# Reordered closing work in a cached attention decode step: maxima, last weights and the last half of V

## Chip, cores, metric

One core of a Trainium2 chip. The profile's span, from first to last instruction, is about 1.9 us shorter than that time.

## The reference

```python
# A_x (1,1,448); A_k_cache, A_v_cache (1,16,65536,256); all bf16
x  = A_x
xn = _layernorm(x)
q  = (xn @ wq) split into 16 heads of 256
p  = softmax(q . k_cache * 256**-0.5)          # over 65536 keys, per head
s  = (p . v_cache, heads side by side) @ wo    # 4096 x 448
g  = silu(silu(xn @ w1) @ w2)                  # the gate
return x + s * g
```

One query against 16 heads of 65536 keys: 1.07 GB of keys and values are read once, with hardly any reuse.

## The kernel before

K and V stream through three large buffers in blocks of 16384 keys of one head (64 blocks of 8 MB each for K and for V). VectorE and ScalarE form the scores, ScalarE the exponentials, and TensorE multiplies them with V. The rows of each block are joined at the end through their maxima and sums. The change concerns only what follows the loops: the last blocks, whose V comes in pieces, and the output projection, whose weights `wo` come in pieces too.

```python
vn = cuts(0, 32, 64, 96, 128)                 # V of the last block but one, in pieces (keys per partition)
vz = cuts(0, 32, 64, 96, 112, 120, 128)       # V of the last block
pieces = cuts(0, 5, 10, 14, 16)               # wo, by heads
# order of the transfers (SP, one queue):
#   K last (2 halves), vn 0..3, vz 0..1, wo 0, wo 1, vz 2.., wo 2, wo 3
...
def pe_rows():    # maxima of the partitions put into one row (L330 before)
def pe_bcast():   # the maximum sent to all partitions (L336)
def pe_turn():    # the O row, copied out of PSUM by act_out, turned into columns (L346)
def pe_keys():    # V matmuls, 128 x 2 x 512 (L318)
def project():    # 1 x 448 projections with wo, two for a head (L681)
...
pe_block(NBLK - 3, 0)
pe_turn()
pe_v(1)                                  # V of the block before, all 128 keys
pe_max(NBLK - 2)                         # pe_rows, query, pe_bcast
...
keys(psO, 2, 2, vn, nl, 0, 3, True)      # keys() waits for each piece, then multiplies it
pe_rows()
keys(psO, 2, 2, vn, nl, 3, 4, False, od)
pe_bcast()
... # ScalarE: softmax of the first half of the last block, sums of the second
keys(psO2, 0, 1, vz, zl, 0, 2, True, od)
pe_turn()
pe.wait_ge(wl[0], 16); project(*pieces[0])
pe_rows()
pe.wait_ge(wl[1], 16); project(h0, h0 + 3)
pe_bcast()
project(h0 + 3, h1)
... # softmax of the last half; sums; weights of the last head
keys(psO, 0, 1, vz, zl, 2, 3, True)      # the last half of V: first piece,
pe_turn()                                # a turn between,
keys(psO, 0, 1, vz, zl, 3, len(vz), False, od)
act_out()
pe.wait_ge(wl[2], 16); project(*pieces[2])
pe_turn(tok=True)
... # VectorE: last head's output (L750)
pe.wait_ge(wl[3], 16); project(pieces[3][0], H1)
project(H1, H)                           # then VectorE: * gate, + x; store
```

## Time and profile before

| | before |
|---|---|
| time, three executions | 2524.33 us median (2523.97 to 2526.91) |
| span of the profiled execution | 2520.7 us |
| read from HBM | 1084 MB, 430 GB/s over the span |
| last V piece of 2 MB (keys 64 to 96) lands | 2504.90 us |
| TensorE without idle time | 2504.95 to 2516.63 us |

VectorE is busy 89% of the span, but, as the prediction reads from the page, it is the transfers that set the pace (416 to 436 GB/s in each of the first 39 slices).

### The profile page before, as it was taken

The numbers are of one execution on the slowest core, as the hardware profiler recorded it, in microseconds if no ns is written. First come the engines' busy times: TensorE is split into PE (matmuls) and PEld (weight loads), VectorE is DVE, ScalarE is ACT, GpSimd is POOL, SyncE is SP. The second block draws the span as 40 slices with busy tenths as digits, with TensorE's granted clock in tenths as the row PEclk, the third lists the DMA queues.
The fourth block names the chain that finished last, engine by engine and source line by source line (L and its number), as shares of the span: only waits on it lengthen the run. The fifth ranks groups of instructions, "written<-read, shape, count | busy, mean of one in ns | idle before, by whom it ended". The sixth has DMA issues, their size and how long they took to land. (4 is left out here: it accounts for less than half of the span.)

```text
span 2520.7 us, 29977 instructions
## 1 busy us (share of the span) xinstructions
PE 1198.9 (48%) x5125; PEld 500.4 (20%) x5125; DVE 2233.5 (89%) x10281; ACT 1443.8 (57%) x6992; POOL 2.5 (0%) x13
## 2 busy tenths in 40 slices
PE   3353544545535445445354354453553544535557
PEld 2121211212212112112121121121221211212123
DVE  6989889889898898898898988988989889889897
ACT  4656556556565565565555655655656556556564
POOL 0000000000000000000000000000000000000000
PEclk7676767767767667677676676776767767767779
DMA  9999999999999999999999999999999999999998
GB/s 423 416 433 432 434 436 433 434 433 433 433 433 433 433 434 432 433 434 434 435 436 434 435 436 435 433 433 434 433 433 433 433 433 433 433 433 434 433 432 342
DMA packets 22728, 1084.52 MB, mean 430 GB/s; under 512 B 2354, under 2 KB 4532, under 8 KB 4916
## 3 DMA queue, kind: packets, MB, share of 16 engines
q1 hardware_dynamic: 22706, 1084.30, 99.6%
q8 instruction: 6, 0.10, 0.0%
q14 instruction: 14, 0.11, 0.0%
q10 hardware_dynamic: 2, 0.00, 0.0%
HBM read 1084.29 MB, written 0.00 MB: 430 GB/s over the span
## 5 line engine op out<-in xcount | busy, mean ns | idle before, releaser
L271 ACT ACTIVATE R<-R 128x256 bf16<-128x256 bf16 x3328 | 1330.7, 401 | 698.5 <-ACTq L154 698.5
L249 DVE CUSTOM_DVE_ANT_0 R<-R,qcur 128x256 bf16<-128x256 bf16 x4864 | 1699.8, 416 | 0.0
L318 PE MATMUL bank<-R,PV 128*2 128x512 bf16 x4096 | 1025.5, 417 | 25.3 <-DMA R<-in_A_v_cache_dram 11.5
L238 DVE TENSOR_TENSOR R<-R,qcur 128x3328 bf16<-128x3328 bf16 x256 | 482.6, 1885 | 197.2 <-DVEq L154 197.1
L271 ACT ACTIVATION_READ_ACCUMULATOR R<-R 128x1 f32 x3328 | 620.1, 186 | 0.0
L330 PE MATMUL bank<-ident,rmax 128*1 128x128 bf16 x65 | 17.1, 263 | 1022.4 <-PEq L154 1022.4
L318 PEld LDWEIGHTS bank<-R,PV 128*2 128x2 bf16 x4096 | 365.7, 90 | 657.2 <-issue 207.1
L249 DVE DVE_READ_ACCUMULATOR2_ANT S<- 128x1 f32 x4864 | 379.4, 78 | 0.0
L346 PE MATMUL bank<-eye,O 2*128 2x1 f32 x536 | 97.2, 298 | 239.8 <-PEq L154 239.8
L330 PEld LDWEIGHTS bank<-ident,rmax 128*1 128x1 bf16 x65 | 5.2, 79 | 1026.6 <-issue 1026.2
L346 PEld LDWEIGHTS bank<-eye,O 2*128 2x128 f32 x536 | 93.3, 255 | 257.8 <-issue 257.8
L284 ACT ACTIVATE hist<-bank 128x1 f32 (+1 forms) x65 | 11.1, 171 | 206.3 <-ACTq L154 206.3
L305 ACT COPY hist<-bank 128x2 f32 (+1 forms) x66 | 10.6, 160 | 119.2 <-ACTq L154 119.2
L214 DVE TENSOR_REDUCE gmax<-bank 1x1 bf16<-1x128 f32 x65 | 18.3, 281 | 38.6 <-DVEq L154 38.6
L231 DVE CAST qcur<-bank 128x256 bf16<-128x256 f32 x64 | 27.2, 425 | 16.0 <-DVEq L154 14.3
L297 ACT COPY O<-bank 2x512 f32<-2x512 f32 x67 | 37.4, 559 | 5.7 <-ACTq L154 5.7
L286 ACT ACTIVATE PV<-S,hist 128x128 bf16<-128x128 f32 (+1 forms) x65 | 26.0, 400 | 13.4 <-ACTq L154 13.1
L358 PE MATMUL bank<-q,ident 16*128 16x256 bf16 x63 | 24.4, 387 | 0.0
L224 DVE COPY S<-S 128x128 f32<-128x128 f32 (+1 forms) x65 | 14.7, 226 | 9.5
L225 DVE TENSOR_REDUCE rmax<-S 128x1 bf16<-128x128 f32 (+1 forms) x65 | 18.2, 280 | 0.0
L336 PE MATMUL bank<-gmax,ones_row 1*128 1x1 bf16 x65 | 10.3, 159 | 16.0 <-PEq L154 16.0
L336 PEld LDWEIGHTS bank<-gmax,ones_row 1*128 1x128 bf16 x65 | 6.5, 100 | 33.4 <-issue 33.4
(65 smaller groups left out, 101.8 us busy)
## 6 DMA issues: line engine op xcount, KB each, us to landing
R<-in_A_k_cache_dram SPq DMA_DIRECT2D x4, 4096.0 KB, 24.7
R<-in_A_v_cache_dram SPq DMA_DIRECT2D x7, 2048.0 KB, 24.1
R<-in_A_wq_dram SPq DMA_DIRECT2D x1, 3072.0 KB, 12.9
R<-in_A_wo_dram SPq DMA_DIRECT2D x2, 1120.0 KB, 19.3
R<-in_B_w_dram SPq DMA_DIRECT2D x1, 1568.0 KB, 27.1
R<-in_B_w_dram SPq DMA_DIRECT2D x1, 1344.0 KB, 5.8
R<-in_A_v_cache_dram SPq DMA_DIRECT2D x1, 1024.0 KB, 15.7
R<-in_A_v_cache_dram SPq DMA_DIRECT2D x2, 512.0 KB, 16.9
```

What stands on the lines that cost most here:

```text
L214: dve.reduce_max(out=gmax[0:1, :], in_=ps_m[0:1, :], axis=AX.X).then_inc(gm, 1)
L225: dve.reduce_max(out=rmax[:, :], in_=S[:, c0:c1], axis=AX.X).then_inc(rm, 1)
L231: dve.tensor_copy(out=qcur[:, :], in_=ps_q).then_inc(sd, 1)
L238: m = dve.tensor_tensor(out=pair, in0=pair, in1=qcur[:, None, :].to_broadcast([P, NA, Dh]), op=ALU.mult,)
L249: ins = dve.tensor_tensor_reduce(out=Kv[:, c, :], in0=Kv[:, c, :], in1=qcur[:, :], scale=1.0, scalar=0.0, op0=ALU.mult, op1=ALU.add, accum ...
L271: ins = act.activation(out=prod, in_=prod, func=ACT.Identity, accum_out=S[:, c : c + 1],)
L286: act.activation(out=PV[s][:, c0:c1], in_=S2[:, c0:c1], func=ACT.Exp, bias=col(0, 1), scale=scale, accum_out=col(1, 2),).then_inc(pv, 1)
L297: act.copy(out=O[:, :], in_=po).then_inc(oc, 1)
L318: ins = pe.matmul(po, lhsT=PV[t][:, c : c + 2], rhs=R[s][:, c * Dh : (c + 2) * Dh], start=(start and c == k0), stop=(stop and c == k1 - 2),)
L330: pe.matmul(ps_m[0:1, :], lhsT=rmax[:, 0:1], rhs=ident[:, :], start=True, stop=True).then_inc(tm, 1)
L346: ins = pe.matmul(ps_t[:, a : a + 1], lhsT=Ov[:, j, a, :], rhs=eye2[:, j : j + 1], start=(j == 0), stop=(j == 1),)
L358: pe.matmul(ps_q, lhsT=ident[0:H, at(h)].to_broadcast([H, P]), rhs=q16[:, :], start=True, stop=True,).then_inc(qr, 1)
```

## The change

Its intent is to take work off TensorE's path behind the last large V piece. (1) The row of maxima of the last block's first half is made behind two pieces of V, not three, and its broadcast ahead of the fourth. (2) A turn moves into a wait, and only four projections stand ahead of the row of maxima of the second half, so that the last softmax and the last head's weights are ready sooner, ahead of the gate. (3) The last half of V, cut finer, is multiplied in one go in the order in which it lands, with no turn between; the other turn goes between the projections.

```diff
--- before.py
+++ after.py
@@ -170,7 +170,7 @@
         return tuple(zip(c[:-1], c[1:]))
 
     vn = cuts(0, 32, 64, 96, 128)
-    vz = cuts(0, 32, 64, 96, 112, 120, 128)
+    vz = cuts(0, 32, 64, 80, 96, 112, 120, 128)
     nl = [sem(f"nl{t}") for t in range(len(vn))]
     zl = [sem(f"zl{t}") for t in range(len(vz))]
     pieces = cuts(0, 5, 10, 14, 16)
@@ -706,10 +706,11 @@
                 pe_keys(po, t, s, k0, k1, start and n == a, last and done is not None,
                         done if last else None)
 
-        keys(psO, 2, 2, vn, nl, 0, 3, True)
+        keys(psO, 2, 2, vn, nl, 0, 2, True)
         pe_rows()
+        keys(psO, 2, 2, vn, nl, 2, 3, False)
+        pe_bcast()
         keys(psO, 2, 2, vn, nl, 3, 4, False, od)
-        pe_bcast()
         act_softmax(LAST, 0, 0, HK)
         act_sums(0, 2)
         act_out()
@@ -718,33 +719,33 @@
 
 
         take(pe, pv)
-        keys(psO2, 0, 1, vz, zl, 0, 2, True, od)
+        keys(psO2, 0, 1, vz, zl, 0, 1, True)
         pe_turn()
+        keys(psO2, 0, 1, vz, zl, 1, 2, False, od)
+        act_out(psO2)
         need("pe", t_o)
         pe.wait_ge(wl[0], 16)
-        project(*pieces[0])
+        (h0, h1) = pieces[0]
+        project(h0, h0 + 2)
         pe_rows()
-        pe.wait_ge(wl[1], 16)
-        (h0, h1) = pieces[1]
-        project(h0, h0 + 3)
+        project(h0 + 2, h1)
         pe_bcast()
-        project(h0 + 3, h1)
         act_softmax(LAST + 1, 0, HK, KB)
-
+        pe_turn()
         take(pe, pv)
         t15 = pe_sums(ps_m[:, 0:NL], N1, NENT)
         weights(N1, NENT, H1, H, (ps_m[:, 0:NL], t15))
-        act_out(psO2)
-        keys(psO, 0, 1, vz, zl, 2, 3, True)
-        pe_turn()
+        t_r = mark("act", act_row(LAST))
         t_g = silu(g_t, ps_y, g_e, t_y)
-        t = mark("act", act_row(LAST))
-        need("dve", t)
+        need("dve", t_r)
         outputs(N1, NENT - 1, H1, H, NL - 1)
-        keys(psO, 0, 1, vz, zl, 3, len(vz), False, od)
+        pe.wait_ge(wl[1], 16)
+        project(*pieces[1])
+        keys(psO, 0, 1, vz, zl, 2, len(vz), True, od)
         act_out()
         pe.wait_ge(wl[2], 16)
-        project(*pieces[2])
+        (h0, h1) = pieces[2]
+        project(h0, h0 + 2)
         t = pe_turn(tok=True)
         need("dve", t)
         t_l = mark("dve", dve.scalar_tensor_tensor(
@@ -755,6 +756,7 @@
             op0=ALU.mult,
             op1=ALU.add,
         ))
+        project(h0 + 2, h1)
         pe.wait_ge(wl[3], 16)
         project(pieces[3][0], H1)
         need("pe", t_l)
```

## The prediction

> **What bounds the kernel now.** I read the page first, then the chain that ended last, then TensorE's timeline of the last 30 us, then the issues and landings of the last transfers.
>
> The page, part 2 (40 slices of 63 us each):
>
> ```profile
> DMA  9999999999999999999999999999999999999998
> GB/s 423 416 433 432 434 436 433 434 433 433 433 433 433 433 434 432 433 434 434 435 436 434 435 436 435 433 433 434 433 433 433 433 433 433 433 433 434 433 432 342
> ```
>
> All 39 first slices move 416 to 436 GB/s with the DMA engines 90% busy or more. 1084 MB must be read (keys and values), and the change moves no byte of it. So about 2504 of 2520.7 us of the span stand, whatever the engines do; only the tail behind the last transfers can shrink. The chain that ended last shows the tail:
>
> ```profile
> 2479.93 24.97 DMA R<-in_A_v_cache_dram
> 2504.91 0.04 issue
> 2504.95 3.61 PE bank L318 x16
> 2508.57 1.03 PE bank L346 x8
> 2509.59 3.54 PE bank L318 x16
> 2513.14 1.51 PE bank L681 x8
> 2514.65 1.03 PE bank L346 x8
> 2515.68 0.95 PE bank L681 x4
> 2516.63 0.02 issue
> 2516.66 0.62 DVE R L763
> 2517.28 0.02 issue
> 2517.30 0.61 DVE x_f L765
> ```
>
> The third piece of the last V block (keys 64 to 96, 2 MB) lands at 2504.90. From there TensorE is never idle until 2516.6: 16 V matmuls, a "turn" (the O row turned into columns, L346), 16 more V matmuls, 8 projections (L681), a second turn, 4 projections. Then two VectorE steps and the store, 4.0 us to the end. TensorE, not DMA, sets these 11.7 us. TensorE's timeline just before it:
>
> ```profile
> 2494.02 3.61 PE L318 MATMUL bank<-R,PV 128*2 128x512 bf16 x16 [2.34 <-DMA R<-in_A_v_cache_dram]
> 2497.56 1.10 PE L346 MATMUL bank<-eye,O 2*128 2x1 f32 x8
> 2498.59 2.05 PE L681 MATMUL bank<-R,OT 128*1 128x448 bf16 x10
> 2500.48 0.22 PE L330 MATMUL bank<-ident,rmax 128*1 128x128 bf16 x1
> 2500.54 1.30 PE L681 MATMUL bank<-R,OT 128*1 128x448 bf16 x6
> 2501.77 0.17 PE L336 MATMUL bank<-gmax,ones_row 1*128 1x1 bf16 x1
> ```
>
> The row of maxima (L330) runs at 2500.48, though VectorE's timeline has its input (L225) finished at 2499.60: it stood behind a turn and ten projections. The broadcast (L336) stood behind six more, although the maximum was ready at 2501.13.
>
> The last transfers: the two V pieces' halves of 512 KB land 16.5 and 17.2 us after their issues (about 2492.2 and 2492.7), so at 2508.7 and 2509.9; the 1 MB piece before them (issued 2491.65, 15.7 us) at 2507.35. The output weights `wl[2]`, issued at 2493.20:
>
> ```profile
> DMA to landing us min/median/max: 18.9/18.9/18.9
> ```
>
> land at 2512.1, and `wl[3]` (issued 2494.3) at 2513.2. In the kernel before nobody waits for them: TensorE reaches them at 2513.14. The stretches show why they are so late:
>
> ```profile
> 2510.50:2511.00 0.50, 0.50 (x4) 0.17 (x2) 0.00 (x0) 0.00 (x0) 0.00 (x0) 1.00 0.18 68
> 2511.00:2512.20 1.20, 1.20 (x7) 0.50 (x6) 0.00 (x0) 0.00 (x0) 0.00 (x0) 1.00 0.07 25
> ```
>
> The DMA share is 0.07, about one engine of 16[...].
>
> [...] the trace has 2507.35 - 2504.90 = 2.45 us, and I use that. [...] The trace's 3.54 us for 16 is 221 ns at clock 1.00[...]. [...]
>
> **The change part by part.** Work is nearly constant: 32 V matmuls, 20 projections, all turns remain; no turn is added or removed, but one leaves the tail.
>
> Step 1, maxima of the last block's first half. They go behind two pieces of V instead of three: L330 at about 2479.1 (its input ends 2478.98) instead of 2481.73. VectorE waited 0.40 us at L214 for it; it now starts the second half 0.40 us earlier, so the second half's maxima end near 2499.2. The broadcast goes ahead of the fourth piece, so ScalarE's softmax starts near 2483 instead of 2487.0; it removes ScalarE as a limit (it ends its sums about 1 us sooner), but VectorE's 0.40 is all that reaches TensorE. Estimates.
>
> Step 2, the last weights. The psO turn goes into the wait before 2494.02 (idle there is 2.34 us, it needs 1.03): free. Only 4 projections remain ahead of L330 (2497.6 to 2498.4), so L330 is bound by its input: 2499.25, gain 1.2 us. Then 6 projections to about 2500.6 and the broadcast at 2500.65 instead of 2501.77. ScalarE's softmax then ends near 2501.7; the turn of psO2 fits beside it (2500.8 to 2501.8). The sums matmul L668 follows at 2501.85 (2502.94 before) and ends about 2502.2. The ten projections of `pieces[1]`, now behind it: 10 x 0.19 = 1.9 us, to 2504.1.
>
> Step 3, the V half in landing order. The split pieces land at 2504.90 - 2.45 = 2502.45 and at 2504.90. TensorE starts 32 matmuls at 2504.1 with no turn among them: 32 x 0.221 = 7.1 us, to 2511.2. Each piece is there when needed: the second at 2505.9 (lands 2504.9), the third at 2507.6 (2507.35, tight), the last two at 2509.4 and 2510.3 (2508.7, 2509.9). Before, this ended at 2513.14: gain 1.9 us, of which 1.03 is the turn and 0.85 the earlier start.
>
> Step 4, the new wait. At 2511.2 TensorE meets `wl[2]`, which lands at 2512.1: 0.9 us idle, so half of step 3 is given back. The copy of O (L297, 0.57 us) hides in it. Then 4 projections 0.75, turn 1.03, 4 projections 0.75 (VectorE's L751, 0.23 us, hides behind them), 2 with `wl[3]` 0.38, the last 2 0.38: 3.3 us, with 0.05 for waits to 2515.5. Before: 2516.63. **Sum: 1.1 us earlier**, and the 4.0 us behind it stand. VectorE's silu, 2.94 us of it the reciprocal, ends about 2508 and is not in the way.
>
> 2524.33 - 1.1 = 2523.2 us, 0.04%.
>
> **The rivals.**
> (a) No DMA wait takes the place: if TensorE alone set the tail, it would end at 2511.2 + 3.3 = 2514.5, gain 2.1 us, 2522.2. Against it: the landing at 2512.1, which the order of transfers doesn't change.
> (b) [...] The waits before V pieces end at 2478.28, 2483.17, 2488.07, 4.9 us apart, but the next at 2494.02, 5.95[...]. One such loss more or one at another place, or the cost of one more transfer, moves `wl[2]`'s landing by about as much: gain 0 to 0.1, 2524.2; one less, gain near 2, 2522.3.
> (c) The earlier weights don't come: if VectorE, or L330's new place behind fewer projections, leaves L668 at 2502.94, the ten projections end at 2505.2, V at 2512.3, after `wl[2]`; the tail ends at 2515.6. Then still 1.0 us. This makes the estimate robust: steps 1 and 2 are nearly hidden by step 4.
> (d) Softer effects: TensorE's clock falls in the added idle time before L330. It is 1.00 from 2480 on, with idle times over 2 us, so I give this little weight.
>
> **Range and chances.** The effect lies between 0 and 2 us. The three runs before spread from 2523.97 to 2526.91, and the profiled one took 2522.64: run to run noise is larger than the effect. So 2523.2, with 2521.5 to 2525.3 for 8 in 10. Faster or slower by 2% means 50 us, which no part of a 40 us closing can give unless the stream of transfers itself is disturbed, and it is untouched: faster 0.003, same 0.992, slower 0.005.
>
> **What would show it right or wrong.** Page part 2 unchanged in its first 39 slices. L330 near 2479.1 and 2499.3, L668 near 2501.9, the V matmuls of the last half in one stretch of about 7.1 us without a turn, from about 2504.1; then an idle time of TensorE near 0.9 us ahead of L681 put down to `in_A_wo_dram`; a chain that ended last which now begins with that transfer instead of V's; last L681 ending near 2515.5. If the wait is not there, (a); if it is longer than 1.5 us and the span is not shorter, (b); if L668 is late, (c). A change above 5 us either way, or slices of lower GB/s, would mean that the closing disturbs the transfers in a way I have not seen.

The sum is 1.1 us, worked with 2.45 us between two landings of the trace (of the 2 MB piece at 2504.90 and of the 1 MB piece at 2507.35) and with 221 ns for a V matmul.

## More of the kernel before

The metric is the device time of one execution in microseconds.

The page's first part (busy time of each engine) and the TensorE clock in the 40 slices of its second part:

```profile
PE 1198.9 (48%) x5125; PEld 500.4 (20%) x5125; DVE 2233.5 (89%) x10281; ACT 1443.8 (57%) x6992; POOL 2.5 (0%) x13
PEclk7676767767767667677676676776767767767779
```

The clock row is in tenths of full speed: TensorE runs at 0.711 in the mean of the span, and is busy for 48% of it.

## The result and the profile after

2523.26 us median of four (2521.99 to 2526.62), before 2524.15 (2523.65 to 2526.91). The ratio is 0.9996, with a 95% interval from 0.9979 to 1.0014: the same, as forecast. The 0.9 us between the medians is about the size forecast (1.1), but smaller than the spread of either kernel. The traces had to show whether it came in the way foretold.

The chain that ended last, in the first profile of the changed kernel (in order of time: start us, us, what; the two steps of VectorE at its end are left out):

```profile
2495.02 17.86 DMA R<-in_A_wo_dram
2512.87 0.04 issue
2512.92 0.92 PE bank L681 x4
2513.84 1.03 PE bank L346 x8
2514.86 2.67 PE bank L681 x8
2517.53 0.02 issue
```

TensorE's timeline before it:

```profile
2494.68 3.61 PE L318 MATMUL bank<-R,PV 128*2 128x512 bf16 x16 [0.27 <-DMA R<-in_A_v_cache_dram]
2499.05 0.22 PE L330 MATMUL bank<-ident,rmax 128*1 128x128 bf16 x1
...
2501.50 0.36 PE L668 MATMUL bank<-hist,ones_sq 128*128 128x5 f32 x2
...
2503.68 3.87 PE L318 MATMUL bank<-R,PV 128*2 128x512 bf16 x16
2508.18 3.61 PE L318 MATMUL bank<-R,PV 128*2 128x512 bf16 x16 [0.64 <-DMA R<-in_A_v_cache_dram]
2512.92 0.92 PE L681 MATMUL bank<-R,OT 128*1 128x448 bf16 x4 [1.12 <-DMA R<-in_A_wo_dram]
```

The order came as meant. The row of maxima is at 2499.05 (2500.48 before), the sums at 2501.50 (2502.94), and the last half of V begins at 2503.68 (2504.95), has no turn in it, and is done about 2511.8 (2513.1). The chain now begins with the output weights, for which TensorE waits 1.12 us. But the last projections end at 2517.53, and before at 2516.63. Part of that is a later arrival of everything: the piece with keys 32 to 64, the same transfer in both kernels, was there at 2494.68 and at 2494.02. To compare profiles I therefore measure the **stretch**: from the start of the V matmuls on keys 32 to 64, which every kernel here but one (told below) begins when they land, to the end of the last projection. Before it is 2516.63 - 2494.02 = 22.61 us, in this profile 22.85: nothing gained. The last eight projections take 2.67 us, where 1.51 had been forecast, and the profile by stretches says why (busy time of the engines, then TensorE's clock in the third column from the right):

```profile
2514.00:2515.00 1.00, 1.00 (x10) 0.88 (x10) 0.01 (x1) 0.00 (x0) 0.00 (x0) 1.00 0.00 0
2515.00:2516.00 1.00, 1.00 (x5) 0.41 (x4) 0.21 (x1) 0.00 (x0) 0.00 (x0) 0.63 0.00 0
2516.00:2517.50 1.50, 1.50 (x5) 0.26 (x2) 0.00 (x0) 0.00 (x0) 0.00 (x0) 0.50 0.00 0
```

The granted clock falls to half at about 2515.3, 2.3 us behind the end of the new wait. Before, it stayed at 1.00 until TensorE was done. The traces of these two kernels show two values of the clock, 1.00 and 0.50, and in each of them all 128 spans from one change to the next are whole multiples of 3.41 us. What TensorE did in such stretches is read from the traces below. This gave a theory and its rivals, at this point my guesses.

**Theory A**: the wait of 1.1 us that the change makes lowers the clock, and the fall costs 1.2 us, all the gain. **Rival B**: it was a chance of that one profile, of where these stretches of 3.41 us fell in the work. **Rival C**: turns and one-row projections lower it, not the wait. Beside these there was the question which of the three parts helps at all, and why single executions are slow.

### The profile page after: what moved, and what is told of

Read it like the earlier page. It is cut to its first block, busy times and chain, and to the rows that moved or that the text cites. A ratio compares the mean times of both kernels' runs of the same rounds, so it can differ in the third digit from the quotient of the medians.

```text
span 2521.6 us, 29978 instructions
## 1 busy us (share of the span) xinstructions
PE 1203.5 (48%) x5125; PEld 501.3 (20%) x5125; DVE 2233.6 (89%) x10281; ACT 1443.9 (57%) x6992; POOL 2.5 (0%) x13
## 5 line engine op out<-in xcount | busy, mean ns | idle before, releaser
L330 PE MATMUL bank<-ident,rmax 128*1 128x128 bf16 x65 | 17.1, 263 | 1022.1 <-PEq L154 1022.0
L249 DVE DVE_READ_ACCUMULATOR2_ANT S<- 128x1 f32 x4864 | 385.8, 79 | 0.0
L330 PEld LDWEIGHTS bank<-ident,rmax 128*1 128x1 bf16 x65 | 5.2, 79 | 1027.0 <-issue 1026.9
```

The costliest lines, as they stand in the source:

```text
L249: ins = dve.tensor_tensor_reduce(out=Kv[:, c, :], in0=Kv[:, c, :], in1=qcur[:, :], scale=1.0, scalar=0.0, op0=ALU.mult, op1=ALU.add, accum ...
L330: pe.matmul(ps_m[0:1, :], lhsT=rmax[:, 0:1], rhs=ident[:, :], start=True, stop=True).then_inc(tm, 1)
```

## The experiments

| kernel | executions, us | median | before, median of the same call | stretch in the profile, us |
|---|---|---|---|---|
| before | (4 in the first call, 9 in each other) | | | 22.61 |
| changed, first profile | 4 | 2523.26 | 2524.15 | 22.85 (clock fell) |
| changed, again | 5 | 2522.13 | 2523.39 | 21.77 |
| wait filled | 5 | 2522.50 | 2523.39 | 21.84 |
| weights split | 5 | 2521.31 | 2523.39 | 20.75 |
| weights split, again | 5 | 2521.49 | 2523.16 | 20.60 |
| split, idle times filled | 5 | 2521.33 | 2523.16 | 21.28 |
| split, earlier maxima | 5 | 2521.30 | 2523.22 | 20.70 |
| long wait | 1 | 2525.70 | 2523.16 | 24.96 (clock fell) |
| long wait filled | 1 | 2524.51 | 2523.16 | 23.58 |
| third part alone | 1 | 2522.60 | 2523.39 | 22.19 (clock fell earlier) |
| third part alone, again | 1 | 2522.67 | 2523.22 | 21.94 |
| first two parts alone | 1 | 2524.24 | 2523.22 | 22.64 |

All gave correct results. Kernels are compared only within the same rounds. Every timed comparison has an interval that contains 1, as single slow executions of 2 to 4 us spread both sides. The profiles are few: the kernel before has one, and the two of the split kernel, which is the same twice, differ by 0.15 us.

**The changed kernel again.** No edit.

> The changed kernel unaltered, to see whether its profile repeats. Theory A (the wait for the output weights of the third piece lowers the granted TensorE clock to half, and the last eight projections take 2.7 instead of 1.5 us): again an idle time near 1.1 us ahead of the projections and the clock at 0.5 in their last microsecond; from the start of the V matmuls of keys 32 to 64 to the end of the last projection 22.8 us, as in the first profile of the changed kernel (22.85; 22.61 before). Rival B[...]: the clock stays at 1.00 and the same stretch takes 21.6 us. Time 2523 +- 1 us, 0 to 1 us under the kernel before.

The end of its chain:

```profile
2512.54 0.92 PE bank L681 x4
2513.46 1.03 PE bank L346 x8
2514.49 1.62 PE bank L681 x8
```

The same wait (1.15 us), and the clock stayed at 1.00: the last eight projections took 1.62 us, the stretch 21.77. So the wait doesn't lower the clock each time: Theory A's numbers missed, Rival B's held (21.6). What was left of A: that the wait makes the fall possible. This is what the change is worth when the clock stays at 1.00: 22.61 - 21.77 = 0.84 us.

**The wait filled.** Five matmuls whose result nobody reads, into a bank that is free by then:

```diff
+for _ in range(5):
+    pe.matmul(bank[7][0:2, :], lhsT=PV[0][:, 0:2], rhs=R[1][:, 0 : 2 * Dh], start=True, stop=True)
 pe.wait_ge(wl[2], 16)
```

> Five V matmuls with no use are written to a free bank ahead of the wait for the third piece of output weights, 5 x 0.221 = 1.1 us, in the idle time. Theory A: the clock stays at 1.00 to the end, the last eight projections take 1.5 us, and the stretch from the V matmuls of keys 32 to 64 to the last projection takes 21.6 to 21.8 us, 1.1 us less than in the changed kernel; time about 2522. If the clock falls because of the turns and the one-row projections and not because of the wait (rival C), it falls here too and the stretch stays at 22.8.

Clock 1.00 to the end, stretch 21.84, eight projections in 1.62 us. That agrees with Theory A, but as the unfilled kernel had just shown the same, it tells nothing apart. A larger dose was needed.

**A longer wait, unfilled and filled.** TensorE waits for the fourth piece of `wo` ahead of the projections of the third; in the second kernel ten unread matmuls stand ahead of it.

```diff
+# second kernel only: 10 matmuls as above
 pe.wait_ge(wl[2], 16)
+pe.wait_ge(wl[3], 16)
```

> The changed kernel with the wait made longer: TensorE waits for the fourth piece of output weights too, before the projections of the third, so it is idle 2.2 to 2.3 us instead of 1.1. Theory A: the clock falls to 0.5[...], and the 3.3 us of work behind the wait take 4.3 us or more. If the throttle doesn't answer to the wait, they take 3.3 us at clock 1.00 and the stretch from the V matmuls of keys 32 to 64 is 22.8 us.

> The same long wait, filled with ten V matmuls of no use (2.2 us). Theory A: the clock stays at 1.00, the 3.3 us of work take 3.3 us and the stretch is 22.8 us. Rival C (turns and one-row projections lower the clock): the same as with the unfilled wait.

TensorE's timeline behind the wait, unfilled:

```profile
2514.01 0.92 PE L681 MATMUL bank<-R,OT 128*1 128x448 bf16 x4 [2.33 <-DMA R<-in_A_wo_dram]
2514.86 1.70 PE L346 MATMUL bank<-eye,O 2*128 2x1 f32 x8
2516.49 3.15 PE L681 MATMUL bank<-R,OT 128*1 128x448 bf16 x8
```

and filled:

```profile
2514.92 0.92 PE L681 MATMUL bank<-R,OT 128*1 128x448 bf16 x4
2515.77 1.10 PE L346 MATMUL bank<-eye,O 2*128 2x1 f32 x8
2516.80 1.68 PE L681 MATMUL bank<-R,OT 128*1 128x448 bf16 x8
```

The same twelve projections and turn took 5.64 us behind 2.33 us of idle time, with the clock at 0.5 from 2515.1 on, and 3.57 us behind busy matmuls, at 1.00. The turns and one-row projections are the same, so they alone don't lower it. (The filled kernel's stretch, 23.58, missed its 22.8: in that execution the last V matmuls began late for a reason told below, and the unread ones ran to 2515.09, while the DMA share was 0.00 from 2514.0 on.) The pair isn't clean, as in the filled kernel that late start had also taken away the 0.61 us of idle time between the V matmuls.

The traces tell more. As the clock changes only at multiples of 3.41 us, each trace can be cut into windows of that length, counted back from its last change. V matmuls of 512 columns start 216 ns apart at clock 1.00, 0.42 ns a column; with that, a streaming time can be added up from the packed traces for each window: columns times 0.42 ns (twice that at clock 0.50). In the traces of the kernel before and of the changed kernel's first profile, 603 windows are at full clock. All 130 with 1.232 us of streaming or less were followed by half clock, and all 473 with 1.247 us or more by full clock. That is a count of these two traces, not a limit tested by a run. The windows at the wait, of the changed kernel's first profile (two lines; the second up to the last projection) and of its second profile (two lines):

```profile
2511.85:2515.26 3.41, 2.34 (x15) 1.51 (x16) 0.23 (x1) 0.57 (x1) 0.00 (x0) 1.00 0.03 13
2515.26:2517.53 2.27, 2.26 (x7) 0.51 (x4) 0.00 (x0) 0.00 (x0) 0.00 (x0) 0.50 0.00 0
2508.81:2512.22 3.41, 2.58 (x12) 0.78 (x10) 0.00 (x0) 0.57 (x1) 0.00 (x0) 1.00 0.51 189
2512.22:2515.63 3.41, 3.09 (x19) 1.85 (x20) 0.23 (x1) 0.00 (x0) 0.00 (x0) 1.00 0.02 7
```

In the first profile 1.07 us of the wait and the whole turn (1.03 us, matmuls of one column, which add next to nothing to the count) lie in one window, and 1.22 us of streaming are left. In the second a window ends inside the wait, and its two windows hold 2.41 and 1.97 us. So by this count, at a wait of 1.1 us it is neither the wait (Theory A) nor the turn (Rival C) alone, but both in one window, and where the windows lie decides that (Rival B). In the unfilled long wait, whose clock fell at 2515.1, 2.32 us of idle time lie in one window with 0.75 us of streaming, so there, by the count, the wait is enough. No run here sets the windows' place. By the same count (an estimate from its trace) the kernel before can lose the clock too: a window that ended between 2504.61 and 2506.18 would have put its last V matmuls at half.

**The output weights split.** If the wait is the bound, its landing should be moved, not filled.

```diff
-pieces = cuts(0, 5, 10, 14, 16)
+pieces = cuts(0, 5, 10, 12, 14, 16)
 ...
 pe.wait_ge(wl[2], 16)
-project(h0, h0 + 2); pe_turn; project(h0 + 2, h1); wait wl[3]; project(14, 15)
+project(10, 12);     pe_turn; wait wl[3]; project(12, 14);     wait wl[4]; project(14, 15)
```

> The third piece of output weights (4 heads) is loaded as two of 2 heads, and TensorE waits for the first of them only, ahead of the turn. Theory A: the first lands about 1.1 us sooner, so there is hardly any idle time, the clock stays at 1.00, and the stretch takes 20.9 to 21.4 us (TensorE without a break, 2 x 0.75 + 1.03 + 0.75 us behind V). That is 1.5 to 2 us under the changed kernel; time about 2521.5. Rival C: the clock falls all the same.

```profile
2508.05 3.62 PE L318 MATMUL bank<-R,PV 128*2 128x512 bf16 x16 [0.64 <-DMA R<-in_A_v_cache_dram]
2511.72 0.92 PE L682 MATMUL bank<-R,OT 128*1 128x448 bf16 x4
2512.57 1.10 PE L346 MATMUL bank<-eye,O 2*128 2x1 f32 x8
```

TensorE goes from V to the projections with 0.05 us between; the landing still comes last (2511.68 in the chain), but now with the end of V. The stretch is 20.75, one microsecond under the change at full clock, a little better than expected. The wait was what step 4 of the prediction had called it: the half of the gain that is given back. The three quick executions were at 2521.3 (quick ones of the change at 2522.0), two of five at 2525.1.

**Split again, and split with all idle times filled.** The same kernel once more to count slow executions, and one with 4, 9 and 2 unread matmuls ahead of the fourth piece of `vn`, the first of `vz`, and the third quarter of the last half of V.

```diff
 pe_bcast()
+warm(2, 2, 4)                            # unread matmuls, as above
 keys(psO, 2, 2, vn, nl, 3, 4, False, od)
+warm(2, 2, 9)
 ...
-keys(psO, 0, 1, vz, zl, 2, len(vz), True, od)
+keys(psO, 0, 1, vz, zl, 2, 4, True)
+warm(0, 1, 2)
+keys(psO, 0, 1, vz, zl, 4, len(vz), False, od)
```

> The split version unaltered, again, to count the slow executions. Theory A: as before one to three of five at about 2525, the rest at 2521.3; in the profile, if it is a slow one, the clock at 0.5 in the closing. Rival E (the two of five were chance, tied to the moment on the chip): the slow ones fall in the same rounds as the kernel before's, or none.

> The version with the split output weights, with matmuls of no use (4, 9 and 2) in the three idle times that TensorE has left in the closing work, ahead of the fourth piece of the V block before, of the first piece of the last V and of the third quarter of it. Theory A (a dip of the granted clock in the closing[...] makes some executions slow): no slow executions, all five within 0.5 us of 2521.3, and the stretch from the V matmuls of keys 32 to 64 to the last projection 20.7 us as in the split version. Rival D (the slow executions come from the transfers or elsewhere): one or two of five at 2524 to 2525 again.

None of ten executions was above 2522.1, and stretches were 20.60 and 21.28. The first split run had two slow ones, so nothing is settled: Theory A foretold slow ones in the unfilled kernel, and there were none; the kernel before had three of nine above 2524. The 21.28 has other causes. In that profile the row of maxima stood at 2500.42, because VectorE had entered the last block late, and two of the unread matmuls (0.43 us) found no idle time left and lengthened the last V. (Its stretch is also the one that doesn't begin with the landing: TensorE came to keys 32 to 64 at 2494.80, and had no wait for them.) The filled long wait had the late VectorE too, and this kernel's VectorE timeline shows where it began:

```profile
2458.64 0.28 DVE L225 TENSOR_REDUCE rmax<-S 128x1 bf16<-128x128 f32 x1
2462.01 0.28 DVE L214 TENSOR_REDUCE gmax<-bank 1x1 bf16<-1x128 f32 x1 [3.09 <-DVEq L154]
```

VectorE waits 3.09 us there for a row of maxima that stands behind all V matmuls of an earlier block on TensorE. That wait was 0.73 to 3.09 us in the profiles before this point (2.24 in the kernel before), and it goes with how long those matmuls stay at half clock in the two profiles compared for it: in the changed kernel's first one the clock rose to full at 2447.0, the 64 matmuls took 15.27 us and VectorE waited 1.35 us; in the kernel before it rose at 2448.5, they took 16.55 us and VectorE waited 2.24 us.

**Maxima between the V matmuls.** The split version, with that row of maxima moved:

```diff
 pe_turn()
-pe_v(1)
-pe_max(NBLK - 2)
+take(pe, pv); take(pe, vl[1], 16)
+pe_keys(psO, 1, 1, 0, 104, True, False)
+pe_rows(); pe_query(NBLK - 1)
+pe_keys(psO, 1, 1, 104, 116, False, False)
+pe_bcast()
+pe_keys(psO, 1, 1, 116, KB, False, True, od)
+pe_mark().then_inc(vf[1], 1)
```

> The split version, with the maxima, query and broadcast of the last block but one put between the V matmuls of the block before it (behind 104 and 116 of 128 keys) instead of behind all of them. Theory F (VectorE waits there 0.7 to 3.1 us, by how long the clock was at half during those V matmuls; when it waits long, VectorE enters the last block late and the tail follows it, not the transfers: so come slow executions): VectorE's wait at L214 in that place falls to 1.0 us or less, the row of maxima of the last half at 2499 or earlier, and the five runs lie within 0.6 us of 2521.2. Rival D (transfers make the slow executions): one of five or more at 2524 to 2525. The fastest runs gain 0 to 0.4 us on the split version, as these are bound by the landing of the weights.

The wait fell to 0.51 us, the row of maxima of the last half came at 2498.48, and five executions lay between 2520.98 and 2521.89. The stretch, 20.70, is that of the split version: VectorE is in time, and the chain that ended last begins with the transfer of `wo`, over at 2511.36, so in this profile a transfer bounds the end. The kernel before had two of nine at 2526.6 and 2527.6. Five quick ones are in accord with Theory F but don't show it, as the split version had five of five quick as well. Why single executions are slow **stays open**; the profiles that I have are all of quick or middling ones.

**Which part helps.** The third part alone (kernel before with `vz` cut as in the change, the last half of V in one `keys` call, and the turn that stood in it moved ahead of the sums), twice; and the change without it.

```diff
 # third part alone, against the kernel before
-vz = cuts(0, 32, 64, 96, 112, 120, 128)
+vz = cuts(0, 32, 64, 80, 96, 112, 120, 128)
 ...
+act_out(psO2)                            # behind the turn of psO
 ...
+pe_turn()                                # ahead of the sums
 take(pe, pv)
 ...
-keys(psO, 0, 1, vz, zl, 2, 3, True); pe_turn(); keys(psO, 0, 1, vz, zl, 3, len(vz), False, od)
+keys(psO, 0, 1, vz, zl, 2, len(vz), True, od)
 ... # ScalarE's last row ahead of the gate, as in the change

 # first two parts alone, against the changed kernel: the same lines the other way round
```

> The kernel before with the third part alone: the V half in landing order, the turn between its pieces moved ahead of the last weights; the maxima stay in their old places. If the first two parts are hidden by the wait for the output weights, as I predicted, the V matmuls end within 0.3 us of the changed kernel's (17.0 us from the start of the V matmuls of keys 32 to 64) or are waiting for the last V piece, and the stretch takes about as long as the changed kernel's: 22.8 us with the clock fallen, 21.6 without.

> The kernel with the third part alone once more, as its first profile had the clock at half in the V matmuls of keys 32 to 64 (5.19 instead of 3.61 us). With the clock at 1.00: V's last matmul ends 17.0 to 17.3 us after those of keys 32 to 64 began, TensorE waits for the output weights 0.5 to 1.0 us, and the stretch takes 21.6 to 21.9 us, as the whole change does: the first two parts add nothing that shows.

> The changed kernel without its third part: maxima and last weights early, but the turn again between the pieces of the V half, which is cut as before. By the prediction's working the first two parts alone are hidden behind the landing of the V piece of keys 64 to 96: TensorE waits for it (0.5 to 1.5 us), then 3.54 + 1.03 + 3.54 us, and the stretch from the V matmuls of keys 32 to 64 takes 22.2 to 22.6 us, against 22.6 before and 21.7 to 21.8 with all three parts at full clock. If it takes 21.8 or less, the first two parts are what helps.

In the first profile of the third part alone the clock fell as the V matmuls of keys 32 to 64 began, behind an idle time of 2.45 us (they took 5.19 us, not 3.61). The kernel before has an idle time of 2.34 us in that place and kept its clock. The count of streaming tells them apart: here, by an estimate from the timeline, 2.26 us of the idle time lie in one window, with 0.99 us of streaming; there a window ends inside it, and the two hold 2.02 and 2.30 us. Even so the stretch was 22.19. The second profile kept the clock: 21.94. TensorE's timeline there:

```profile
2504.75 7.07 PE L318 MATMUL bank<-R,PV 128*2 128x512 bf16 x32
2512.98 1.67 PE L681 MATMUL bank<-R,OT 128*1 128x448 bf16 x8 [1.17 <-DMA R<-in_A_wo_dram]
```

All 32 matmuls in one run, then the same wait for `wo`. The change without its third part:

```profile
2506.52 3.61 PE L318 MATMUL bank<-R,PV 128*2 128x512 bf16 x16 [1.40 <-DMA R<-in_A_v_cache_dram]
2510.06 1.10 PE L346 MATMUL bank<-eye,O 2*128 2x1 f32 x8
2511.09 3.61 PE L318 MATMUL bank<-R,PV 128*2 128x512 bf16 x16
```

TensorE is ready 1.40 us before the 2 MB piece lands, and from there all is as before: 22.64 against 22.61. So the third part alone takes 0.67 of the 0.84 us, the first two alone nothing, as the prediction's working had it. Whether they add anything to the third isn't shown: with it alone V ends 17.1 us into the stretch and the wait is 1.17 us, as in the whole change, and the 0.17 us left (0.1 in the order of work behind the landing, 0.08 in the landing) are about what two profiles of one kernel differ by.

## Why the prediction was right, and where it was not

The time was right: 2523.26 for 2523.2, and the same within 2%. That rests on the first paragraph of the prediction, that the stream of 1084 MB sets 2504 us and is not touched. The nearness to 0.1 us is luck, as the runs spread over several us. By its steps:

- **Step 1** held: L330 at 2478.90 (forecast 2479.1), the last half's maxima sooner, and by the first two parts alone it gives nothing at the end.
- **Step 2** held: L330 at 2499.05 (2499.25), sums at 2501.50 (2501.85), V from 2503.68 (2504.1). The first two parts alone measured no gain, so rival (c), "Then still 1.0 us" without the earlier weights, was right in kind: 0.67.
- **Step 3** held in kind. The matmuls came without a turn, but TensorE waited 0.64 us for the piece called tight. Counted from the start of the stretch that piece landed 0.1 us later than forecast, and TensorE came to it 0.7 us sooner. So V ended 17.1 us into the stretch, hardly before the forecast 2511.2 - 2494.02 = 17.2, though it had begun 1.1 us sooner: the landings took that back.
- **Step 4** held in its wait: 1.12 and 1.15 us for `wl[2]`, forecast 0.9, and the chain that begins with it. What follows was mis-sized: "3.3 us, with 0.05 for waits to 2515.5", measured 3.56 us at full clock (0.92 + 1.03 + 1.62 us in the chain). With that 0.2 us and a landing 0.1 us later in the stretch, the gain is 0.84 us and not 1.1.
- **Rival (d)** was wrongly set aside: "TensorE's clock falls in the added idle time", named for the idle time ahead of L330, happened at the wait for `wl[2]`, in one of two profiles, and cost 2.67 - 1.62 = 1.05 us, more than the gain. The reason given, that the clock had stayed at 1.00 with idle times over 2 us, was too weak: the longest, 2.34 us, had been cut by the end of a window (2.02 and 2.30 us of streaming in the two), and the third part alone lost its clock behind 2.45 us in the same place. Here a turn of 1.03 us stands behind a shorter wait of 1.12 us.
- **Rival (b)**, a later landing, came in part: the landing of keys 32 to 64 was 0.66 us later in the first profile of the changed kernel than before, and 0.31 in the second, which no step of the change explains. What delayed it isn't shown: the line with a DMA share of 0.07 tells only of the last of `wo`.

## What to carry to other kernels

Behind a stream of transfers, taking work off an engine ends at the next landing (here in a wait of 1.12 us for `wo`): look up when everything needed later arrives before counting a gain, and if a wait takes the place of the work, split or reorder that transfer (here one more cut in the weights gave a further 1.0 us of the stretch). Look at what a new idle time of TensorE does to its clock behind it, together with the small matmuls beside it (here 1.12 us and a turn of 1.03 us, with the clock at 0.50 behind them in one of two profiles), and don't judge it from one profile. Effects of a microsecond beside an execution-to-execution spread of three are to be read from a stretch of the trace that begins with the same event in both kernels.
